# Turned w_out blocks in one PSUM bank with one copy, the first group's logits one piece later, the output's split ahead of the state's sum

## The chip, the cores and the metric

The kernel runs on one core of a Trainium2 chip. The metric is the device time of one execution in microseconds (us). A core has five engines, each with its own in-order queue: PE (TensorE, matrix products; its weight loads are shown as PEld), DVE (VectorE), ACT (ScalarE), POOL (GpSimd) and SP (SyncE, which here only issues DMAs). An engine's next instruction waits behind the one before it. PE writes its results to PSUM, which has eight banks; DVE and ACT read them there, POOL can't.

## What is computed

Three layers, one after the other, on 3072 tokens of width 384.

```
# 1. a linear-attention recurrence over 768 steps (4 batches, 8 heads of 48)
cur   = (u * k_t) outer v_t
y_t   = r_t @ (state + cur)
state = w * state + k_t outer v_t
# 2. a feed-forward layer
h = x @ w_in          # 384 -> 2048
x = maximum(0.01 * h, h) @ w_out      # 2048 -> 384
# 3. routing to one of 8 experts, for tokens with a positive score
score, logits = x @ w_skip, x @ w_gate
e = argmax(logits);  gate = softmax(logits)[e]
out = x + gate * (relu(x @ w1[e]) @ w2[e])     # where score > 0, else out = x
```

## The kernel before, in words

**Number format.** Every product runs in f16 with two parts: a value is split into a high part and a rest, and three products (high by high, rest by high, high by rest) are added in PSUM. "The split" is such a pair: ACT rounds to f16, DVE (or POOL) subtracts.

**Tiling.** The attention runs in 24 steps i of 128 tokens, each in two chunks c of 64. Three steps make a group g of 384 tokens, eight groups in all. One step consists of these functions: `att_S` (PE, line 334, the products of k and r), `take_S` (DVE, L343, the masked copy into `dg`), `att_V` (PE, L358, a chunk's contribution to the state), `next_T` (DVE, L374 adds it to the decayed state `Tw`, L376 decays the sum again), `att_Y` (PE, L391), `att_R` (PE, L406, the state's share of the output) and `take_y` (for each chunk ACT L424 and DVE L425: the output's split into `xt`). From step 8 on, S uses banks 0 and 1, and V, Y and R of both chunks use banks 2 and 3: Y and R the columns below 256, V those above. The listings call banks 0 to 7 bank_85 to bank_92. Some waits between engines are kept by bank, not by column: in the listing of the kernel before, the second L424 waits for the state's sum, which reads other columns of the same bank.

**The feed-forward layer.** `mm1` (L477 to L479) makes 9 products of 384 columns per block f of 16, `mm2` (L505 to L507) 12 per piece q of four f. `mm1` ends in ACT L482 and DVE L483, then ACT L492 and L493 on DVE or POOL. The end of mm2 is ACT L529 and L530 and DVE L533.

**The opening (0 to about 148 us).** Its order is written out by hand: a string `SEQ` of letters, one for each small function, which all engines follow. While attention runs for the first steps, the weights come in as 64-bit words and are converted: 16 chunks of w_in, then 16 of w_out, each by four DVE operations or three and POOL (letters B, C, X, l or h: L202, L205, L210, then L216 on DVE, or L218 on ACT and L219 on POOL) and ACT L211. Letter x is `turn_w_out`: it transposes block c of w_out, three 128x128 tiles of the high part and three of the rest, by PE (L752) into the two banks of `idle_pair()` (the pair that attention isn't using: bank_87 and bank_88, later bank_85 and bank_86), and ACT copies each bank to `slotE` (L753). Letter f is `fuse_logits`: four turned blocks times the router's weights (PE L234, L235), so that mm2 can give the router's nine logits as nine more columns of w_out (393 columns in place of 384). Letter 2 is one f of the first group's mm2, for which w_out block f must be there.

**After the opening.** A loop over groups g issues mm1 and mm2. `tick()` counts pieces, and on every fourth `pump()` issues half an attention step: S of step i with R of step i-1 and, for the engines behind them, `take_S`, `next_T`, `take_y` in `att_posts`; four ticks later V and Y. The first group has no logits from mm2, since the fused columns weren't ready: `first_logits()` computes them from `xT0`, the group's rows turned by three DMAs on SP (L914). It is called in group 1, i = 0, after piece q = 2. `routing(g)` then works on the logits in small steps, one per piece. After the groups come the experts.

Of the kernel before, what the change touches and what calls it, by code (L numbers as in the profile page):

```python
# [10 lines left out]
F16 = mybir.dt.float16  # L11
# [7 lines left out]
P = 128  # L19
# [10 lines left out]
NK = DM // P  # L30
# [30 lines left out]
def kernel(ctx: ExitStack, tc: tile.TileContext, rk, nat, wT, uN, w_in, w_out, wsg,  # L61
                         w1, w2, c_diag, c_mask, c_id48, c_f16, c_route, c_tok, out):
    nc = tc.nc
    v, act, g_, pe, sp = nc.vector, nc.scalar, nc.gpsimd, nc.tensor, nc.sync
# [19 lines left out]
    def ring(k):  # L84
        turns[k] = turns.get(k, -1) + 1
        if k == "mm":
            return bank[4 + turns[k] % state["ring"]]
        return bank[turns[k] % 2][:, 256:]
# [157 lines left out]
    def fuse_logits(c):  # L246

        whole()
        pl = idle_pair()[c % 2] if state["seq"] else ring("at")
        for j in range(4):  # L250
            for k in range(NK):
                two_parts(pl, j, slotE[:, 0, 4 * c + j, k, :], slotE[:, 1, 4 * c + j, k, :], wsg_s[:, :, k, :],
                          k == 0, k == NK - 1)
        fl = rt.tile([P, 4, 9], F32, name="fl")
        add_parts(fl, pl, 4)
        split(w_out_s[:, 0, 4 * c:4 * c + 4, DM:NX], w_out_s[:, 1, 4 * c:4 * c + 4, DM:NX], fl, 1.0 / SR)
# [60 lines left out]
    def idle_pair():  # L317

        i = done["s"]
        assert i - done["e"] < 2 and done["t"] >= 2 * i - 2  # L320
        return bank[2 * (i % 2):2 * (i % 2) + 2]
# [120 lines left out]
    def pump():  # L442

        i = done["y"]
        if done["s"] == i and (i < NST or done["r"] < NST):
            if i < NST:
                if done["c"] <= i:
                    sum_c()
                if done["d"] <= i:
                    set_diag(g_)  # L450
                att_S()
                att_posts.append(take_S)
            if done["r"] < i:
                att_R()
                if done["t"] < 2 * i:
                    att_posts.append(next_T)
                att_posts.append(take_y)
        elif i < NST:
            if i + 1 < NST:
                for x, f in (("a", scale_rk), ("u", mul_ruk), ("n", scale_k)):  # L460
                    if done[x] <= i + 1:
                        f(g_)
            if done["v"] == i:
                att_V()
            att_Y()
            if done["t"] == 2 * i:
                att_posts.append(next_T)
# [276 lines left out]
    def turn_w_out():  # L744

        c = turn("x")
        assert ready["w"] > NF + c
        whole()
        for h, b in enumerate(idle_pair()):
            tp = b[:, :NK * P // 2].bitcast(F16)  # L750
            for k in range(NK):
                pe.transpose(tp[:, k * P:(k + 1) * P], w_out_s[:, h, c, k * P:(k + 1) * P], ident16)  # L752
            act.copy(slotE[:, h, c].rearrange("p k n -> p (k n)"), tp)  # L753

    posts = []

# [104 lines left out]
    for g in range(NG):  # L861
# [54 lines left out]
        for i in range(TPG):  # L916
            st = {}
            for q in range(4):
                tick()
                whole()  # L920
                post = mm2(g, gT, i, 4 * q, 4 * q + 4, st, DM if last else NX)
                if g == 1 and i == 0:

                    held, post = post, None
                skew(post)
                flush()
                if last:
                    if i == 0:
                        if q == 0:
                            for f in range(NF - 3, NF):  # L930
                                late_logits(g, gT, f, bank[3])
                            rts = routing(g)
                        for _ in range(2 if q == 1 else 1):
                            next(rts, None)
                        if q == 1:
                            for k in range(NB2):
                                if k != buf_of(E0, 0):
                                    g_.memset(xg_b[k], 0.0)
                    if (i, q) in ((1, 0), (1, 1), (2, 1)):
                        next(cnts)  # L940
                    if i < 2:
                        split_pieces(1)
                elif g == 1:
                    if i == 0:
                        if q == 2:
                            first_logits()
                        if q == 3:
                            rts = routing(0)
                    else:
                        next(rts, None)  # L950
                    if (i, q) == (1, 3):
                        for j in range(TPG):
                            store_x(0, j)
                        held()
                elif q % 2:
                    if early < 16:
                        pieces.append(load_expert(early // 8, early % 8, stg, NST4))
                        early += 1
                    if len(pieces) > 2 or (pieces and early == 16):
                        pieces.pop(0)()  # L960
# [225 lines left out]
```

## Time and profile before

| | |
|---|---|
| median of three runs | 640.87 us (640.70 to 642.69) |
| the profiled execution | 639.15 us, span 637.3 us from first to last instruction |
| busy share of the span | PE 95%, DVE 66%, ACT 40%, POOL 40% |
| mean granted TensorE clock | 0.991 of full speed |

How to read it: busy times are shares of the span of one profiled execution. PE's busy time is a union of overlapping matmuls (a 384-column matmul lasts 0.33 us but the next starts 0.16 us later). An idle time is written in brackets behind the instruction that ended it, with the instruction that released it. Idle time of an engine other than the one that sets the pace costs nothing by itself.

### The profile page before, as it was taken

The numbers are of one execution on the slowest core, as the hardware profiler recorded it, in microseconds if no ns is written. First come the engines' busy times: TensorE is split into PE (matmuls) and PEld (weight loads), VectorE is DVE, ScalarE is ACT, GpSimd is POOL, SyncE is SP. The second block draws the span as 40 slices with busy tenths as digits, with TensorE's granted clock in tenths as the row PEclk, the third lists the DMA queues.
The fourth block names the chain that finished last, engine by engine and source line by source line (L and its number), as shares of the span: only waits on it lengthen the run. The fifth ranks groups of instructions, "written<-read, shape, count | busy, mean of one in ns | idle before, by whom it ended". The sixth has DMA issues, their size and how long they took to land.

```text
span 637.3 us, 17708 instructions
## 1 busy us (share of the span) xinstructions
PE 603.0 (95%) x7116; PEld 393.1 (62%) x7116; DVE 417.6 (66%) x907; ACT 255.4 (40%) x539; POOL 253.5 (40%) x242
## 2 busy tenths in 40 slices
PE   8899988988999999999999999999999999999994
PEld 4456555655656666665666666666566677777772
DVE  7999988863278738956884892583177363473751
ACT  1236656552045225433642541252155242352530
POOL 3958654543542624544262454421013323221310
PEclk9989999999999999999999999999999999999998
DMA  8867354623632652553263243003155755797750
GB/s 266 252 198 224 91 159 141 192 67 76 138 117 77 169 163 100 155 169 111 68 171 118 89 120 101 14 2 90 35 180 176 242 141 156 238 213 213 188 152 12
DMA packets 60350, 89.04 MB, mean 140 GB/s; under 512 B 20706, under 2 KB 44224, under 8 KB 60240
## 3 DMA queue, kind: packets, MB, share of 16 engines
q1 hardware_dynamic: 56784, 81.64, 44.6%
q0 software_dynamic: 2880, 5.49, 2.9%
q8 instruction: 66, 1.08, 0.7%
q10 hardware_dynamic: 576, 0.47, 0.2%
q14 instruction: 44, 0.36, 0.2%
HBM read 68.86 MB, written 17.23 MB: 135 GB/s over the span
## 4 chain that ended last, share of the span: by engine, by line
PE 50%; DMA 15%; DVE 14%; issue 12%; POOL 5%; ACT 2%; POOLq 0%; SPq 0%; DVEq 0%; ACTq 0%
PE bank L505 8%; PE bank L507 8%; PE bank L506 8%; PE bank L477 7%; PE bank L478 7%; PE bank L479 7%; DMA idxl<-tokid,su 6%; DMA out_x<-y,idx 3%; DMA xg<-xbuf,idx 3%; DVE wc L210 2%; PE bank L406 2%; DVE bank L202 2%; DVE bank L205 2%; PE bank L358 1%; PE bank L334 1%
## 5 line engine op out<-in xcount | busy, mean ns | idle before, releaser
L477 PE MATMUL bank<-xt,slotA 128*128 128x384 f16 x384 | 125.4, 326 | 2.4 <-DVE gg L483 2.3
L479 PE MATMUL bank<-xt,slotA 128*128 128x384 f16 x384 | 125.2, 326 | 0.0
L478 PE MATMUL bank<-xt,slotA 128*128 128x384 f16 x384 | 125.2, 326 | 0.0
L505 PE MATMUL bank<-slotB,slotC 128*128 128x393 f16 (+1 forms) x336 | 110.7, 329 | 0.0
L507 PE MATMUL bank<-slotB,slotC 128*128 128x393 f16 (+1 forms) x336 | 110.5, 329 | 0.0
L506 PE MATMUL bank<-slotB,slotC 128*128 128x393 f16 (+1 forms) x336 | 110.5, 329 | 0.0
L483 DVE TENSOR_TENSOR gg<-bank,gg 128x384 f32<-128x384 f32 x128 | 70.2, 551 | 30.6 <-ACT gg L482 30.3
L482 ACT ACTIVATE gg<-bank 128x384 f32<-128x384 f32 x128 | 61.9, 489 | 60.0 <-PE bank L479 42.6
L493 DVE TENSOR_TENSOR slotC<-gg,slotC 128x384 f16<-128x384 f32 x101 | 78.5, 780 | 0.2
L298 POOL TENSOR_TENSOR dg<-cs,diag 128x512 f32<-128x512 f32 x21 | 22.2, 1057 | 130.9 <-DVE cs L291 130.9
L492 ACT CAST slotC<-gg 128x384 f16<-128x384 f32 x112 | 56.8, 508 | 15.5 <-DVE gg L483 14.8
L533 DVE SCALAR_TENSOR_TENSOR x<-bank,x 128x384 f16<-128x384 f32 x24 | 13.2, 557 | 72.4 <-ACT x L530 69.1
L270 POOL TENSOR_TENSOR raw<-raw,consts 112x512 f32<-112x512 f32 x44 | 56.8, 1315 | 0.1
L478 PEld LDWEIGHTS <-slotA 128*128 128x128 f16 x384 | 37.5, 98 | 25.0 <-issue 3.1
L479 PEld LDWEIGHTS <-slotA 128*128 128x128 f16 x384 | 37.5, 98 | 24.9
L477 PEld LDWEIGHTS <-slotA 128*128 128x128 f16 x384 | 37.4, 97 | 23.8
L529 ACT ACTIVATE x<-bank 128x384 f16<-128x384 f32 x24 | 11.8, 492 | 92.4 <-PE bank L507 79.2
L507 PEld LDWEIGHTS <-slotC 128*128 128x128 f16 x336 | 32.9, 98 | 22.7
L505 PEld LDWEIGHTS <-slotC 128*128 128x128 f16 x336 | 32.8, 98 | 21.9
L506 PEld LDWEIGHTS <-slotC 128*128 128x128 f16 x336 | 32.9, 98 | 20.7
L590 POOL DMA_INDIRECT idxl<-tokid,su x24 | 25.7, 1069 | 50.1 <-DVE s L594 39.6
L992 ACT ACTIVATE h<-bank 128x512 f16<-128x512 f32 x28 | 16.7, 596 | 60.4 <-PE bank L986 44.3
(211 smaller groups left out, 1284.4 us busy)
## 6 DMA issues: line engine op xcount, KB each, us to landing
raw<-in_w SPq DMA_DIRECT2D x48, 384.0 KB, 5.7
raw<-in_nat SPq DMA_DIRECT2D x24, 576.0 KB, 5.8
raw<-in_rk SPq DMA_DIRECT2D x24, 448.0 KB, 4.0
xbuf<-x SPq DMA_DIRECT2D x23, 384.5 KB, 5.8
wst<-in_w_in SPq DMA_DIRECT2D x16, 384.0 KB, 6.7
wst<-in_w_out SPq DMA_DIRECT2D x16, 384.0 KB, 3.5
wst<-in_w SPq DMA_DIRECT2D x16, 384.0 KB, 5.6
out_x<-x SPq DMA_DIRECT2D x24, 192.0 KB, 1.9
```

The source lines that it names most:

```text
L270: eng.tensor_mul(r4[:, a], r4[:, a], tab.unsqueeze(2).broadcast_to([112, NPAIR, 2, C]))
L477: pe.matmul(ph[:, :n], wh, xt[:, 0, k, t0:t0 + n], start=k == 0, stop=False)
L478: pe.matmul(ph[:, :n], wh, xt[:, 1, k, t0:t0 + n], start=False, stop=False)
L479: pe.matmul(ph[:, :n], wl, xt[:, 0, k, t0:t0 + n], start=False, stop=k == NK - 1)
L482: act.activation(gg[:, :n], ph[:, :n], AF.Copy, scale=0.01)
L483: v.tensor_max(gg[:, :n], ph[:, :n], gg[:, :n])
L492: act.copy(gT[:, 0, f, t0:t0 + n], gg[:, :n])
L493: eng.tensor_sub(gT[:, 1, f, t0:t0 + n], gg[:, :n], gT[:, 0, f, t0:t0 + n])
L505: pe.matmul(po[:, :c1 - c0], gh, w_out_s[:, 0, f, c0:c1], start=start, stop=False)
L506: pe.matmul(po[:, :c1 - c0], gh, w_out_s[:, 1, f, c0:c1], start=False, stop=False)
L507: pe.matmul(po[:, :c1 - c0], gl, w_out_s[:, 0, f, c0:c1], start=False, stop=stop)
L590: g_.indirect_dma_start(out=idxl[i], out_offset=bass.IndirectOffsetOnAxis(ap=su[:, i:i + 1], axis=0), in_=tokid[:, ti:ti + 1], in_offset=N ...
```

## The change

Three edits. First, `turn_w_out`: where no V of the step ahead has been issued into the idle pair (`done["v"] <= done["s"]`), all six transposes of block c go into one bank, bank c % 2 of the pair, 768 f16 columns wide, and one ACT copy of 2x384 columns takes both parts to `slotE`. 13 of the 16 blocks are turned so; blocks 3, 4 and 5 keep two half banks and two copies. `fuse_logits` writes to the bank of the block turned last. Second, `first_logits()` is called after piece q = 3. Third, in `pump()` the split `take_y` stands ahead of `next_T`, the state's sum.

```
-        pl = idle_pair()[c % 2] if state["seq"] else ring("at")
+        pl = idle_pair()[(done["x"] + 1) % 2] if state["seq"] else ring("at")
...
                 att_R()
+                att_posts.append(take_y)
                 if done["t"] < 2 * i:
                     att_posts.append(next_T)
-                att_posts.append(take_y)
...
-        for h, b in enumerate(idle_pair()):
-            tp = b[:, :NK * P // 2].bitcast(F16)
+        banks = idle_pair()
+        whole_bank = done["v"] <= done["s"]
+        tps = ([banks[c % 2][:, :NK * P].bitcast(F16)] if whole_bank else
+               [b[:, :NK * P // 2].bitcast(F16) for b in banks])
+        for h in range(2):
+            tp = tps[0][:, h * NK * P:] if whole_bank else tps[h]
             for k in range(NK):
                 pe.transpose(tp[:, k * P:(k + 1) * P], w_out_s[:, h, c, k * P:(k + 1) * P], ident16)
-            act.copy(slotE[:, h, c].rearrange("p k n -> p (k n)"), tp)
+            if not whole_bank:
+                act.copy(slotE[:, h, c].rearrange("p k n -> p (k n)"), tp)
+        if whole_bank:
+            act.copy(slotE[:, :, c].rearrange("p h k n -> p h (k n)"), tps[0].rearrange("p (h n) -> p h n", h=2))
...
-                        if q == 2:
+                        if q == 3:
                             first_logits()
-                        if q == 3:
                             rts = routing(0)
```

On ACT, near the end of the opening (blocks 9 to 13; L211 and L218 belong to the conversion of later chunks, wc is their staging tile), before:

```order
L753 COPY slotE_140<-bank0_85 128x384
L753 COPY slotE_140<-bank1_86 128x384
L753 COPY slotE_140<-bank0_85 128x384
L753 COPY slotE_140<-bank1_86 128x384
L211 ACTIVATE slotB_137<-wc_1895 128x384
L753 COPY slotE_140<-bank0_85 128x384
L753 COPY slotE_140<-bank1_86 128x384
L753 COPY slotE_140<-bank0_85 128x384
L753 COPY slotE_140<-bank1_86 128x384
L211 ACTIVATE slotB_137<-wc_1956 128x384
```

And after:

```order
L492 CAST slotD_139<-gg_1501 128x384
L760 COPY slotE_140<-bank1_86 128x2x384
L760 COPY slotE_140<-bank0_85 128x2x384
L211 ACTIVATE slotB_137<-wc_1887 128x384
L760 COPY slotE_140<-bank1_86 128x2x384
L760 COPY slotE_140<-bank0_85 128x2x384
L211 ACTIVATE slotB_137<-wc_1946 128x384
L218 ACTIVATE wc_1946<-wc_1946 128x384
```

Each pair of copies became one, and two blocks in a row no longer share a bank.

On DVE, the end of step 9 in group 2 (dg and S's banks 85, 86; T, Tw the state; xt the output's two parts; gg the mm1 result), before:

```order
L493 TENSOR_TENSOR slotC<-gg,slotC 128x384
L343 COPY_PREDICATED dg<-mask,bank_85 128x256
L343 COPY_PREDICATED dg<-mask,bank_86 128x256
L374 TENSOR_TENSOR T<-Tw,bank_88 112x192
L376 TENSOR_TENSOR Tw<-T,pw 112x192
L425 SCALAR_TENSOR_TENSOR xt<-bank_87,xt 112x4x64
L425 SCALAR_TENSOR_TENSOR xt<-bank_88,xt 112x4x64
L483 TENSOR_TENSOR gg<-bank_90,gg 128x384
```

And after:

```order
L493 TENSOR_TENSOR slotC<-gg,slotC 128x384
L343 COPY_PREDICATED dg<-mask,bank_85 128x256
L343 COPY_PREDICATED dg<-mask,bank_86 128x256
L425 SCALAR_TENSOR_TENSOR xt<-bank_87,xt 112x4x64
L425 SCALAR_TENSOR_TENSOR xt<-bank_88,xt 112x4x64
L374 TENSOR_TENSOR T<-Tw,bank_88 112x192
L376 TENSOR_TENSOR Tw<-T,pw 112x192
L483 TENSOR_TENSOR gg<-bank_90,gg 128x384
```

The two halves of the output's split moved ahead of the sum and its decay; the rows around them stayed. With that, the second L424 on ACT has no wait for the sum any more.

## Rows read from the trace of the kernel before

**Rows 1.** Stretches: length, busy us (count) by engine, PEclk, DMA share, GB/s.

```profile
100.00:120.00 20.00, 17.77 (x243) 11.66 (x243) 17.01 (x40) 11.38 (x30) 9.95 (x10) 1.00 0.52 156
...
200.00:220.00 20.00, 20.00 (x218) 12.45 (x217) 15.80 (x38) 7.99 (x19) 10.95 (x10) 1.00 0.50 128
...
560.00:580.00 20.00, 19.22 (x250) 15.89 (x250) 10.50 (x15) 6.82 (x11) 5.58 (x5) 1.00 1.04 245
```

**Rows 2.** Waits of PE, 90 to 150 us: total, times, longest.

```profile
PE bank L752 <- ACT slotE L753: 4.4, 5, 1.6
PE bank L234 <- ACT slotE L753: 1.0, 2, 0.6
```

**Rows 3.** Waits of PE, 150 to 485 us.

```profile
PE bank L358 <- POOL ru L278: 1.6, 2, 0.8
PE bank L234 <- DMA slotE<-x: 1.2, 1, 1.2
PE bank L358 <- DVE xt L425: 0.8, 1, 0.8
```

**Rows 4.** PE in order of time, turns and fused logits: start, length, idle before.

```profile
101.41 0.71 PE L752 MATMUL bank<-cf,slotB 128*128 128x128 f16 x6 [1.60 <-ACT slotE L753]
...
130.35 0.71 PE L752 MATMUL bank<-cf,slotB 128*128 128x128 f16 x6 [1.43 <-ACT slotE L753]
...
138.76 0.17 PE L234 MATMUL bank<-wsg_s,slotE 128*128 128x18 f16 x1 [0.40 <-ACT slotE L753]
```

**Rows 5.** ACT in order of time.

```profile
106.54 0.49 ACT L482 ACTIVATE gg<-bank 128x384 f32<-128x384 f32 x1 [0.91 <-PE bank L479]
...
138.23 0.86 ACT L753 COPY slotE<-bank 128x384 f16<-128x384 f16 x2 [0.83 <-PE bank L752]
```

**Rows 6.** DVE in order of time.

```profile
104.44 0.56 DVE L483 TENSOR_TENSOR gg<-bank,gg 128x384 f32<-128x384 f32 x1 [0.51 <-ACT gg L482]
...
107.06 0.56 DVE L483 TENSOR_TENSOR gg<-bank,gg 128x384 f32<-128x384 f32 x1 [0.84 <-ACT gg L482]
107.53 0.54 DVE L210 SCALAR_TENSOR_TENSOR wc<-wst,bank 128x384 uint32<-128x384 uint32 x1
...
135.69 0.55 DVE L210 SCALAR_TENSOR_TENSOR wc<-wst,bank 128x384 uint32<-128x384 uint32 x1
```

**Rows 7.** Groups by shape: count, busy us, mean ns, idle before.

```profile
L753 ACT COPY slotE<-bank 128x384 f16<-128x384 f16 x32 | 13.6, 476 | 5.0 <-PE bank L752 4.8
...
L992 ACT ACTIVATE h<-bank 128x512 f16<-128x512 f32 x28 | 16.7, 596 | 60.4 <-PE bank L986 44.3 <-issue 12.6 <-ACT slotE L191 1.4
```

**Rows 8.** PE in order of time, the first group's logits.

```profile
155.22 0.17 PE L235 MATMUL bank<-wsg_s,slotE 128*128 128x9 f16 x1
156.56 0.18 PE L234 MATMUL bank<-wsg_s,slotE 128*128 128x18 f16 x1 [1.18 <-DMA slotE<-x]
```

**Rows 9.** DVE, then ACT, at the end of step 9.

```profile
184.94 0.77 DVE L343 COPY_PREDICATED dg<-mask,bank 128x256 f32<-128x256 uint32 x2
185.60 0.34 DVE L374 TENSOR_TENSOR T<-Tw,bank 112x192 f32<-112x192 f32 x1
185.97 1.19 DVE L376 TENSOR_TENSOR Tw<-T,pw 112x192 f32<-112x192 f32 x1
187.09 0.74 DVE L425 SCALAR_TENSOR_TENSOR xt<-bank,xt 112x256 f16<-112x256 f32 x2
...
185.97 0.38 ACT L424 ACTIVATE xt<-bank 112x256 f16<-112x256 f32 x1 [2.32 <-DVE T L374]
```

**Rows 10.** PE, V of steps 9, 10 and 22, and the matmul ahead of one.

```profile
170.67 0.57 PE L358 MATMUL bank<-raw 64*48 64x48 f32 x32
...
186.44 0.33 PE L479 MATMUL bank<-xt,slotA 128*128 128x384 f16 x1
187.60 0.81 PE L358 MATMUL bank<-raw 64*48 64x48 f32 x29 [0.83 <-POOL ru L278]
...
412.12 0.76 PE L358 MATMUL bank<-raw 64*48 64x48 f32 x29 [0.85 <-DVE xt L425]
```

## The prediction

> **What bounds the kernel now.** I read the table of stretches first, then PE's waits, then the rows around each wait. Inside the groups (200 to 220 us) PE is busy for all 20.00 us, DVE for 15.80, ACT for 7.99 [rows 1]: PE sets the pace, and a change is worth what it takes from PE's waits. In the opening it is two engines at once: from 100 to 120 us PE has 17.77 and DVE 17.01 of 20 us [rows 1], both in order, and each sometimes waits for the other. So the next view is who PE waits for. Between 90 and 150 us it is the copies of the turned blocks: 4.4 us in five waits of the transposes and 1.0 us in two of the fused logits [rows 2]. Between 150 and 485 us there are four waits only: 1.2 us for the turned rows of the first group, and three of 0.8 us in front of V [rows 3]. Two of these three are put down to POOL's `ru`, but V at 187.60 comes 0.1 us after the first L425 ends (187.09 and about 0.4 of the pair's 0.74), and its later part after the second [rows 9, 10]; the third row names L425 itself [rows 3, 10]. I take L425 for all three.
>
> **Edit 3, the split ahead of the sum.** At 184.94 DVE does the two masked copies, then the sum (L374, 0.34), the decay (L376, 1.19 here), and only then the two L425, from 187.09 to 187.83; the second L424 on ACT waits 2.32 us for the sum as well [rows 9]. PE is through with mm1 at 186.77 (186.44 and 0.33) and stands 0.83 us [rows 10]. V then also runs torn: its first 29 matmuls take 0.81 us where all 32 take 0.57 at 170.67 [rows 10]; start of V to the end of its last three is about 0.28 us longer. One place costs 1.1 us, three cost 0.83 + 0.81 + 0.85 + 3 x 0.28 = 3.3 us. After the change L425 starts at about 185.6, when L374 started, and the pair ends at 186.35; L374 follows to 186.6, and the long L376 is behind everything that V needs. V on the first bank is free at 186.0 and on the second, whose state columns the sum must have read, at 186.65, when PE arrives at 186.7. Gain 3.3 us; the most that is left is about 0.1 at each place. Nobody else is late: the sum ends before the L425 did, ACT loses a wait, SP's `xt` DMAs behind L425 go earlier.
>
> **Edit 2, logits one piece later.** PE does two thirds of the logits up to 155.22 and begins the last third at 156.56, when the third turning DMA lands [rows 8]: 1.3 us lost beyond the 0.03 pitch. One piece is 12 matmuls at 0.167 us, 2.0 us. Put ahead, it ends at about 157.0, and the last third comes 0.7 us after the data. Gain 1.3 us, and it needs the DMAs to move with PE, which they do, since the rows they turn come from mm2. What goes later: DVE's first routing steps, by 0.8 us on the old clock; the next use of them on PE is a piece later still. Bounds 0.6 (if the DMA stays where it was in time while PE comes 2.7 us earlier) and 1.3.
>
> **Edit 1, the copies.** Its parts in order.
> - Price of a copy: two copies of 384 columns take 0.86 us as a pair [rows 5]. One of 768 isn't in the trace; from 384 columns at 476 ns [rows 7] and the slope between 476 and 596 ns for 128 more (0.94 ns a column at most), 0.80 to 0.84 us. So ACT gains nothing worth a term; 13 instructions go, 40% busy stays. A copy starts after six transposes and not after three, 0.17 us later, which counts where PE waits for it.
> - Block 2 at 101.41 waited 1.60 us for block 1's copies in the same banks [rows 4]. It now goes to the other bank, and PE is 1.6 us earlier, 2.0 with the torn second half. DVE at that time stands for ACT's L482, which stands for PE (106.54 after 0.91 idle [rows 5]; the three L483 at 104.44 to 107.06 after 0.51, 0.66 and 0.84 [rows 6]). With PE ahead these three run at their own pitch of 0.47: 104.4, 104.85, 105.3, and L210 comes at 105.8 in place of 107.53. **DVE gains 1.7 us**, and from there to the last L210 at 135.69 [rows 6] it has hardly an idle place, so it keeps them.
> - From 107 to 128 us PE follows DVE (the copies stand behind ACT's L211, which waits for L210), 1.7 us earlier.
> - Block 10 at 130.35 waited 1.43 us for block 9's copies [rows 4]: gone, PE is 3.1 us ahead, then 3.5 with block 12's 0.4.
> - Then a new wait takes part back. The third fused logits write into the bank of block 13, turned last, and wait for its whole copy. That stands behind the L211 of the last chunk, whose L210 ends at 136.24 - 1.7 = 134.5: L211, then the copy from 135.05 to 135.9. Before, they began at 138.76 [rows 4]: 2.8 us gained, with PE idle for about 2 us ahead of it.
> - Block 15's copy begins after six transposes: 0.1 us lost on the way to `dg` and step 8's end.
>
> Sum of edit 1: **2.7 us**. Lower bound: if DVE doesn't keep the 1.7 us, the third logits come at 137.65 and 1.0 us is left; if alternating gave nothing at all, the full copy (138.23 + 0.84, where the first half was enough) and block 15 would cost 0.4. Upper bound 3.5, without the new wait. I take 2.7: each row on the way names the engine ahead of it.
>
> The page "Perfetto Trace Analysis" of the Trainium skill (section "Optimizing Scalar/DVE Operations") says that grouping operations pays where the engine is saturated, and gives about 51 ns of ScalarE overhead on PSUM. By that, 13 copies less give an estimated 0.7 us on an engine that isn't saturated, and nothing of the time; the rows agree that ACT isn't what is short.
>
> **The sum.** 3.3 + 1.3 + 2.7 = 7.3 us. Against the profiled execution: 639.15 - 7.3 = 631.85 us (span 630.0). The other three runs lie 1.5 to 3.5 us above the profiled one, with the median 640.87, so the forecast for the median is 640.87 - 7.3 = 633.6 us. Bounds of the parts: 3.0 to 3.5, 0.6 to 1.3, -0.4 to 3.5.
>
> **Rivals.**
> - *DVE doesn't keep its lead* (it is at 17 of 20 us, and its operations grow where POOL works beside them): edit 1 gives 1.0, total 5.6, 635.3 us. For it: the length of L376, 1.19 here [rows 9]. Against: DVE's idle places in 104 to 107 us are plainly waits for PE. Chance 0.15.
> - *The wait changes sides.* L424 and the sum read the same bank and can't overlap; now the sum waits for L424 and L425, and V waits for the sum. If the sum (or the decay with it) came as late as the L425 did, the three places would stay: 4.0 us gained, 636.9 us. Against: the 1.19 us decay is behind the sum. Chance 0.08. The page "PSUM — Partial Sum Buffer" of the Trainium skill (section "PSUM bank collisions raise a hardware error") says that two engines must be kept apart on one bank and quadrant, reads against reads included; that is the wait of 2.32 us [rows 9], and by that rule the order is turned and the exclusion stays.
> - *The wins are taken back later.* Between 560 and 580 us the DMA queues show a share of 1.04 [rows 1]. If the experts' weights set the end, an earlier PE waits there, and the time is 640.9 us. Against: PE is busy 19.22 us in that stretch, and the weight loads are issued when buffers are read, so they move with PE. Both this and the first two in part: about 638.5. Chance 0.10 for all of it.
> - *Slower: DVE waits at the head of its queue.* In 13 steps DVE now reaches L425 first, which needs R and ACT, where it used to do sum and decay (0.34 + about 0.36 at least) in that time. If DVE stands 0.7 us in each with the L483 of mm1 behind it, and PE then lacks a free bank, that is 13 x 0.7 = 9.1 us, and V's waits stay: 640.87 - 4.0 + 9.1 = 646.0 us. It decides once L483 is as late as PE's need of the bank; between 150 and 485 us PE waits for no L483 [rows 3], and DVE has some 4 us in 20 to spare [rows 1]. Chance 0.05.
> - *The edits do nothing:* the order of instructions shows each where it is meant to be, so this is only the third rival.
>
> **How the numbers follow.** The forecast, all three parts, has 0.62. The range reaches from 631.0 (all upper bounds, 8.3 us, off the profiled execution) over the first two rivals to 637.5 and leaves out the 0.10 of the third and 0.05 of the slower one. Two versions are told apart from about 0.3%, 1.9 us, so faster means below 638.95: 0.62 + 0.15 + 0.08 and 0.03 of the third rival's partial case, 0.88. Same 0.07, slower 0.05.
>
> **What would show it.** Edit 3: V of steps 10, 16 and 22 at about 182.8, 293.9 and 405.1 us (187.60 less 4.0 and 0.83, then 1.1 more each time) without an idle time, and L425 ahead of L374. Edit 2: no wait for `slotE<-x`. Edit 1: no wait of blocks 2 and 10, the last L210 near 134.0, the third fused logits near 136.0 behind a wait of about 2 us. Wrong would be a last L210 that stays near 135.7 (first rival), V waiting for T (second), new waits of PE in mm1 for L483 (the slower one), or a gain by 450 us that is gone at the end (third).

## The result and the profile after

The changed kernel takes 635.99 us (median of four runs, 634.5 to 637.52) where the kernel before took 641.78 in the same comparison: ratio 0.9895, 95% interval 0.9859 to 0.9932. Two later batches gave 0.9913 (0.9883 to 0.9944) and 0.9878 (0.9846 to 0.9909). So it is about 1% faster, 5.8 us. The forecast was 633.6 us, with a range of 631.0 to 637.5: the direction is right, the time is in the range, and the gain is 1.5 us short of the 7.3 us forecast.

The profiled execution of after took 636.7 us, with a span of 634.8. Its opening ran 2.74 us late before any of the three edits acts: the first block of `w_out` is turned at 94.76 us, against 92.02 before. In fourteen profiles of this study that point lies between 92.0 and 95.1 us. From there up to the third fused logits two profiles of one kernel agree to some hundredths of a microsecond, so below I count from block 0's first transpose. In the changed kernel L756 are the transposes, L758 the half copies, L760 the joined copy, and L477 to L507 the mm1 and mm2 matmuls as before.

The table of stretches of after (length, busy us and count of PE, PEld, DVE, ACT and POOL, then PEclk, DMA share, GB/s):

```profile
100.00:120.00 20.00, 18.96 (x255) 12.45 (x253) 18.66 (x43) 12.66 (x31) 11.56 (x12) 1.00 0.57 177
139.00:142.00 3.00, 3.00 (x23) 1.79 (x20) 1.32 (x5) 0.24 (x1) 0.00 (x0) 0.59 0.20 80
142.00:145.00 3.00, 3.00 (x23) 1.90 (x22) 0.00 (x0) 1.28 (x2) 0.00 (x0) 0.84 0.00 0
200.00:220.00 20.00, 20.00 (x218) 12.41 (x217) 15.75 (x37) 7.92 (x17) 11.93 (x11) 1.00 0.46 115
```

Against [rows 1], PE and DVE both work more of the stretch from 100 to 120 us, and the groups are as they were. New at this place is PEclk, the granted share of TensorE's full clock: 0.59 and 0.84 between 139 and 145 us. PE counts as busy there for every microsecond, and yet it is slow. PE's waits of after between 90 and 150 us (total, times, longest):

```profile
PE bank L234 <- ACT slotE L760: 3.0, 2, 1.8
PE bank L756 <- ACT slotE L758: 0.9, 1, 0.9
PE bank L477 <- DVE gg L483: 0.7, 1, 0.7
PE bank L234 <- DVE dg L343: 0.6, 1, 0.6
```

Of the 4.4 us of the transposes in [rows 2], 0.9 is left, ahead of a block that kept its half banks; the fused logits (L234) went from 1.0 to 3.0 us. From 150 to 485 us the same view of after is empty: all four waits of [rows 3] are gone. PE of after in order of time, at the places of [rows 4], [rows 8] and [rows 10]:

```profile
102.39 0.50 PE L756 MATMUL bank<-cf,slotB 128*128 128x128 f16 x6
...
126.57 0.17 PE L234 MATMUL bank<-wsg_s,slotE 128*128 128x18 f16 x1 [1.21 <-ACT slotE L760]
...
129.34 0.83 PE L756 MATMUL bank<-cf,slotB 128*128 128x128 f16 x12
...
138.46 0.17 PE L234 MATMUL bank<-wsg_s,slotE 128*128 128x18 f16 x1 [1.75 <-ACT slotE L760]
...
139.22 0.32 PE L506 MATMUL bank<-slotB,slotC 128*128 128x384 f16 x1
139.38 0.37 PE L507 MATMUL bank<-slotB,slotC 128*128 128x384 f16 x1
139.55 0.53 PE L505 MATMUL bank<-slotB,slotC 128*128 128x384 f16 x1
139.87 0.53 PE L506 MATMUL bank<-slotB,slotC 128*128 128x384 f16 x1
...
158.41 0.17 PE L234 MATMUL bank<-wsg_s,slotE 128*128 128x18 f16 x1
...
186.84 0.57 PE L358 MATMUL bank<-raw 64*48 64x48 f32 x32
```

Block 2 (102.39) has no wait, blocks 9 and 10 run in one piece of twelve transposes (129.34), the first group's logits (158.41) and V of step 10 (186.84) start without a wait, and V is whole, 32 matmuls in 0.57 us. The third fused logits stand 1.75 us for the copy of the block turned last. Half a microsecond after them the starts of the mm2 matmuls go from 0.16 us apart (139.22, 139.38) to 0.32 (139.55, 139.87), half of the rate, until 142.75. I call this the slow stretch. DVE of after in order of time, the last L210 and the split:

```profile
136.61 0.55 DVE L210 SCALAR_TENSOR_TENSOR wc<-wst,bank 128x384 uint32<-128x384 uint32 x1
...
185.71 0.74 DVE L425 SCALAR_TENSOR_TENSOR xt<-bank,xt 112x256 f16<-112x256 f32 x2
186.37 0.34 DVE L374 TENSOR_TENSOR T<-Tw,bank 112x192 f32<-112x192 f32 x1
186.75 0.53 DVE L376 TENSOR_TENSOR Tw<-T,pw 112x192 f32<-112x192 f32 x1
```

The joined copy's group by shape on ACT (count, busy us, mean ns, idle before):

```profile
L760 ACT COPY slotE<-bank 128x768 f16<-128x768 f16 x13 | 10.0, 793 | 4.3 <-PE bank L756 4.3
```

The last L210 is 1.8 us earlier, counted from block 0 (43.67 to 41.85). The split starts right behind the masked copies, in the place that the sum had before [rows 9], and the sum and the decay follow behind it. A whole copy takes 793 ns, where a pair of halves took 0.86 us [rows 5].

### The profile page after: what moved, and what is told of

It is laid out like the page before. It is cut to its first block, busy times and chain, and to the rows that moved or that the text cites. A ratio compares the mean times of both kernels' runs of the same rounds, so it can differ in the third digit from the quotient of the medians.

```text
span 634.8 us, 17710 instructions
## 1 busy us (share of the span) xinstructions
PE 603.1 (95%) x7116; PEld 392.4 (62%) x7116; DVE 417.3 (66%) x907; ACT 255.4 (40%) x526; POOL 253.9 (40%) x242
## 5 line engine op out<-in xcount | busy, mean ns | idle before, releaser
L477 PE MATMUL bank<-xt,slotA 128*128 128x384 f16 x384 | 125.3, 326 | 3.0 <-DVE gg L483 2.9
L507 PE MATMUL bank<-slotB,slotC 128*128 128x393 f16 (+1 forms) x336 | 111.0, 330 | 0.0
L483 DVE TENSOR_TENSOR gg<-bank,gg 128x384 f32<-128x384 f32 x128 | 70.0, 551 | 27.2 <-ACT gg L482 26.8
L477 PEld LDWEIGHTS <-slotA 128*128 128x128 f16 x384 | 37.5, 98 | 23.8
L529 ACT ACTIVATE x<-bank 128x384 f16<-128x384 f32 x24 | 11.8, 492 | 95.1 <-PE bank L507 75.8
L507 PEld LDWEIGHTS <-slotC 128*128 128x128 f16 x336 | 33.0, 98 | 23.0 <-issue 0.5
```

What stands on the lines that cost most here:

```text
L477: pe.matmul(ph[:, :n], wh, xt[:, 0, k, t0:t0 + n], start=k == 0, stop=False)
L483: v.tensor_max(gg[:, :n], ph[:, :n], gg[:, :n])
L507: pe.matmul(po[:, :c1 - c0], gl, w_out_s[:, 0, f, c0:c1], start=False, stop=stop)
```

## The experiments

Three batches of kernels, the runs of one batch on one chip, and a last run by itself. Times are medians, with the ratio to the kernel before in the same batch:

| kernel | us | before | ratio (95%) |
|---|---|---|---|
| e1, edit 1 alone | 640.95 | 643.44 | 0.9967 (0.9945 to 0.9990) |
| e2, edits 2 and 3 | 639.17 | 643.44 | 0.9928 (0.9901 to 0.9954) |
| e3, logits in the other bank | 632.27 | 643.44 | 0.9829 (0.9800 to 0.9858) |
| e4, wait filled | 635.17 | 643.44 | 0.9866 (0.9839 to 0.9894) |
| e5, changed kernel | 634.27 | 639.53 | 0.9913 (0.9883 to 0.9944) |
| e6, two copies | 633.69 | 639.53 | 0.9905 (0.9879 to 0.9931) |
| e7, one bank | 635.06 | 639.53 | 0.9931 (0.9904 to 0.9957) |
| e8, sum first | 632.62 | 639.53 | 0.9890 (0.9862 to 0.9918) |
| e10, logits in the other bank | 629.16 | 639.95 | 0.9820 (0.9792 to 0.9847) |
| e11, changed kernel | 632.18 | 639.95 | 0.9878 (0.9846 to 0.9909) |
| e12, wait filled | 633.36 | 640.39 | 0.9878 (0.9836 to 0.9920) |

e9, the kernel before, was executed once, for its profile (639.15 us).

The intervals are 3 to 5 us wide, wider than most of the steps in question. The traces are sharper. Each has the same marks, here in us from block 0's first transpose to the start of the mark (of V, to the end of the last one), and in the last column from there to the end of the span:

| profile | block 2 | last L210 | third logits | block 15 | last V | rest |
|---|---|---|---|---|---|---|
| before | 9.39 | 43.67 | 46.74 | 50.60 | 341.92 | 203.4 |
| e9, before | 9.39 | 43.68 | 46.75 | 50.61 | 341.25 | 203.3 |
| e2, edits 2 and 3 | 9.39 | 43.69 | 46.76 | 50.62 | 337.36 | 208.1 |
| e7, one bank | 9.71 | 43.39 | 46.27 | 50.14 | 337.19 | 202.4 |
| after | 7.63 | 41.85 | 43.70 | 49.23 | 335.96 | 204.1 |
| e5, changed kernel | 7.63 | 41.83 | 43.68 | 49.10 | 335.82 | 202.7 |
| e11, changed kernel | 7.63 | 41.82 | 43.67 | 47.53 | 334.43 | 202.7 |
| e1, edit 1 alone | 7.63 | 41.83 | 43.67 | 49.21 | 340.81 | 206.8 |
| e8, sum first | 7.64 | 41.83 | 43.68 | 49.21 | 337.69 | 205.3 |
| e6, two copies | 7.63 | 42.01 | 43.92 | 49.45 | 336.36 | 203.5 |
| e4, wait filled | 7.64 | 41.85 | 43.70 | 47.56 | 334.38 | 206.2 |
| e12, wait filled | 7.63 | 41.83 | 43.68 | 47.54 | 334.64 | 202.4 |
| e3, other bank | 7.63 | 41.49 | 40.42 | 44.28 | 331.35 | 207.1 |
| e10, other bank | 7.63 | 41.48 | 40.42 | 44.28 | 331.38 | 202.3 |

**e1, edit 1 alone.** Edits 2 and 3 undone in the changed kernel.

```
-                att_posts.append(take_y)
                 if done["t"] < 2 * i:
                     att_posts.append(next_T)
+                att_posts.append(take_y)
...
-                        if q == 3:
+                        if q == 2:
                             first_logits()
+                        if q == 3:
```

> Edit 1 alone (edits 2 and 3 undone). Theory (a new wait and then half the clock): the third fused logits stand about 1.7 us for the copy of the block turned last, and about 1 us later the second third of the following mm2 matmuls comes at 0.32 us in place of 0.16 us each, with a granted clock under 0.7 in that 3-us stretch; edit 1 is then worth 1.3 us: time before less 1.0 to 1.6 us, and V of steps 10, 16 and 22 waits 0.8 us each as before. Rival A (the forecast's step, the wait alone and the slow stretch of the after run an accident of that one run): the wait is there, the clock is 1.00 behind it, and 2.7 us or more are gained. Rival B (edit 1 does nothing that lasts): 0 +- 0.4.

Block 15 came 1.39 us earlier than before, the last V 1.11 us. The time's interval (0.6 to 3.5 us gained) holds both theories. The trace doesn't: the wait of 1.76 us is there, and so is the slow clock. The stretch behind the logits in e1:

```profile
138.40:141.40 3.00, 3.00 (x15) 1.82 (x14) 0.86 (x3) 0.80 (x1) 0.00 (x0) 0.50 0.05 18
```

PEclk is 0.50, the lower of the two levels (1.2 of 2.4 GHz). PE's waits from 150 to 485 us are those of [rows 3] again, 1.7 and 0.9 us in front of V and 1.3 us for the turned rows. So the slow stretch of after wasn't an accident of one execution, and edit 1 alone is enough for it to come.

**e2, edits 2 and 3.** The kernel before, with `first_logits()` one piece later and `take_y` ahead of `next_T`; `turn_w_out` and `fuse_logits` as before.

> Edits 2 and 3 on the kernel before (edit 1 undone). Theory: the three V waits gone (3.4 us) and the wait for the first group's turned rows gone (1.2 to 1.3 us): 4.6 to 4.7 us less than before; the clock between the third fused logits and block 15 stays 1.00. If edit 2's DMA stays where it was in time, 4.0 to 4.2. Rival (edit 1 carried part of edit 3's or edit 2's gain, since PE comes earlier there): the difference to before is under 3.5 us.

The last V ends 4.56 us earlier than before (341.92 to 337.36), and the time agrees (ratio 0.9928, 4.6 us). The opening stays as it was to 0.02 us, block 15 at 50.62, PEclk 1.00. V of step 9 starts at 77.36 from block 0 and at 78.65 before, which is edit 2's 1.29 us; the other 3.27 us are edit 3's. The view of PE's waits from 150 to 485 us is empty. The two edits don't lean on edit 1. POOL and PE of e2 at step 10:

```profile
185.74 0.99 POOL L278 TENSOR_TENSOR ru<-ru,consts 128x384 f32<-128x384 f32 x1
```

```profile
186.43 0.59 PE L358 MATMUL bank<-raw 64*48 64x48 f32 x32
```

V starts 0.3 us before POOL's `ru` is finished (186.73), so V doesn't wait for it, although [rows 3] puts two of the three stalls down to it.

**e3, the logits in the other bank.** The changed kernel, with the fused logits not in the bank of the block turned last but in that of the block turned second last.

```
-        pl = idle_pair()[(done["x"] + 1) % 2] if state["seq"] else ring("at")
+        pl = idle_pair()[done["x"] % 2] if state["seq"] else ring("at")
```

> The changed kernel with the fused logits in the other bank of the pair, that of the block turned second last, whose copy is done at about 135.0 us of the changed kernel's profile while PE arrives at 136.7. Theory (the wait costs 1.7 us and the half clock behind it another 1.7 us): third fused logits at about 136.9 in place of 138.46, no wait of over 0.3 us ahead of them, mm2 behind them at 0.16 us, block 15 about 3.3 us earlier than 143.99; 3.0 to 3.4 us less than the changed kernel, so 8.5 to 9.3 us less than before. The second fused logits lose their wait of 1.21 us too, but PE follows DVE there: 0. Rival A (the slow mm2 belong to that stretch itself, whatever stands ahead): 1.6 us less than the changed kernel, clock again under 0.7. Rival B (the time goes into the next wait, for POOL's dg ahead of the fourth logits): the wait of 0.58 us there grows to 2 us or more and under 1 us is gained.

PE of e3, block 13 and the third fused logits:

```profile
132.36 0.50 PE L756 MATMUL bank<-cf,slotB 128*128 128x128 f16 x6
132.69 0.17 PE L234 MATMUL bank<-wsg_s,slotE 128*128 128x18 f16 x1
```

The logits follow the transposes at the transposes' own pace, without a wait, and the clock stays at 1.00. Block 15 comes 4.95 us earlier than in after (49.23 to 44.28), more than the 3.3 us expected: 1.67 to 1.70 us is the half clock (below), and the third logits themselves come 3.28 us earlier, not 1.6. The rest stems from the second fused logits. They lost their wait of 1.21 us too, and blocks 9 and 10 then start at 33.22 instead of 34.58. My expectation put nothing down for that, because I had PE following DVE there. The wait for `dg` ahead of the fourth logits is 0.58 us as in after, so rival B falls.

**e4 and e12, the wait filled.** Seven matmuls that nobody reads, 512 columns each, ahead of the third fused logits; the wait for the copy stays.

```
         assert done["x"] >= 4 * c + 4
+        if c == 2:
+            warm(7, done["x"] % 2, 4 * P)
         fuse_logits(c)
```

> The changed kernel with seven matmuls of 512 columns that nobody reads, into the bank that is free, right ahead of the third fused logits: PE works in its wait of 1.75 us, and the wait for the copy stays where it was. Theory (PE's idle time of 1.75 us is what lowers the clock): the logits start at 138.4 to 138.6 us as before this edit, the mm2 behind them come at 0.16 us, clock 1.00, block 15 at about 142.3 in place of 143.99: 1.4 to 1.8 us less than the changed kernel, 7.2 to 7.6 less than before. Rival (the slow mm2 have another cause): 0 +- 0.3 against the changed kernel, clock again under 0.7.

> The changed kernel with seven unread matmuls in the wait ahead of the third fused logits, a second time, since in one of the three profiles of the changed kernel the half clock did not come although the wait of 1.75 us was there. Over all kernels with that wait empty it came in five of six profiles. Theory (PE's idle time brings it on): none here either, block 15 at 47.5 to 47.6 us from block 0, last V's end at 334.4; by chance alone two filled profiles without it would be 1 in 36. Rival (it comes and goes with that stretch, whatever PE does in the wait): half clock again, block 15 at 49.1 to 49.3. Time: 6.5 to 7.7 us less than before.

PE of e12, then its stretches behind the logits:

```profile
135.60 0.50 PE L756 MATMUL bank<-cf,slotB 128*128 128x128 f16 x6
135.93 1.67 PE L107 MATMUL bank<-wu 128*128 128x512 f16 x7
137.85 0.17 PE L234 MATMUL bank<-wsg_s,slotE 128*128 128x18 f16 x1 [0.24 <-ACT slotE L760]
```

```profile
139.00:142.00 3.00, 3.00 (x28) 2.03 (x27) 1.05 (x4) 1.04 (x2) 0.00 (x0) 1.00 0.13 50
142.00:145.00 3.00, 3.00 (x50) 1.89 (x48) 0.00 (x0) 1.85 (x5) 1.47 (x3) 1.00 0.00 0
```

The logits start at 43.68 from block 0, exactly as in the changed kernel: the copy sets them, whatever PE does. But the clock stays at 1.00, and block 15 is at 47.54 and 47.56 instead of 49.10 to 49.23. PE did useless work, and by block 15 the kernel was 1.6 us ahead of the executions with the slow stretch. The whole times don't show this gain: e12's ratio to before is that of e11, the changed kernel (0.9878 both). The medians are 8.3 us (e4) and 7.0 us (e12) below before, where I had said 7.2 to 7.6 and 6.5 to 7.7.

**e5 and e11, the changed kernel again.**

> The changed kernel once more, with a profile of its own. Counted from block 0 of the turned blocks, which took the opening's variation out of the five profiles seen so far to within 0.03 us: block 2 at 7.63, last L210 at 41.85, third fused logits at 43.70 behind a wait of 1.75, then a stretch of half clock, block 15 at 49.2, last V at 335.4. If the half clock belongs to the wait it comes again; if it was an accident of one run, block 15 is at 47.6. The time from the last V to the end, 203.9 to 208.7 us in the profiles so far, can't be told beforehand; if the changed kernel gave back its gain there, it would be longer than the 203.9 of the kernel before by the 6 us gained, if not, anywhere among these. Time: 5.5 to 7.0 us less than before.

> The changed kernel, for the comparison side by side: from block 0, third fused logits at 43.7 behind a wait of 1.75 us, half clock behind it, block 15 at 49.1 to 49.3, last V's end at 335.8 to 336.0; 5.5 to 6.5 us less than before.

The third fused logits of e11, then one stretch behind the logits from each, e5 first and then e11:

```profile
136.33 0.17 PE L234 MATMUL bank<-wsg_s,slotE 128*128 128x18 f16 x1 [1.75 <-ACT slotE L760]
```

```profile
138.00:141.00 3.00, 3.00 (x14) 1.64 (x13) 1.30 (x5) 0.24 (x1) 0.00 (x0) 0.52 0.10 38
```

```profile
137.00:140.00 3.00, 3.00 (x27) 1.93 (x24) 1.32 (x5) 1.04 (x2) 0.00 (x0) 1.00 0.28 112
```

e5 repeats after. e11 doesn't, and my expectation missed: it has the same wait of 1.75 us and the full clock behind it, block 15 at 47.53, and its median is 7.8 us below before where I had said 5.5 to 6.5. So the same kernel has the slow stretch in some executions and not in others, and 49.10 to 49.23 against 47.53 is what it costs: 1.6 to 1.7 us. Over all kernels that wait there with PE empty (after, e1, e5, e6, e8, e11) it came in five profiles of six, and in none of the eight others. Five in six is a count of profiles and no rate: the mean granted clock of a run, which takes in every low stretch of it, is 0.987 to 0.991 in five of e5's six runs (633.75 to 635.93 us; the sixth has 0.993 and 631.41), and 0.992 or 0.993 in five of e11's six (631.44 to 632.27 us; the sixth has 0.988 and 635.41). With e3 and e10, where the wait is gone, and e4 and e12, where it is filled, I take PE's idle time as what brings it on. For the filling this is argued more than shown: by the counts alone, none of two against five of six comes about by chance once in nine. And the idle time isn't enough for it: e7 has a wait of 1.97 us ahead of other work (below), before has 1.60 and 1.43 [rows 4], all with PEclk at 1.00 behind them. What else decides stays open. The Trainium skill, page "TensorE: Matmul & The Clock Gate" (section "Part 1: The HAM clock gate (the "warmup" mystery)"), says that the clock has only these two levels; the 0.50 of e1 agrees with that. It also says that the number of matmuls that a kernel starts with at the lower one differs from run to run; e5 and e11 differ in a like way, but in the middle of the kernel.

**e6, two copies.** The changed kernel, with its packed and alternating banks, but two copies of 384 columns from each whole bank.

```
-            act.copy(slotE[:, :, c].rearrange("p h k n -> p h (k n)"), tps[0].rearrange("p (h n) -> p h n", h=2))
+            for h in range(2):
+                act.copy(slotE[:, h, c].rearrange("p k n -> p (k n)"), tps[0][:, h * NK * P:(h + 1) * NK * P])
```

> The changed kernel with its packed, alternating banks, but two copies of 384 columns for each whole block in place of one of 768. Theory (alternating the banks is edit 1's gain, joining the copies is worth next to nothing, since ACT is busy for half of the time): block 2 at 7.6 us from block 0, block 15 at 49.2 to 49.5, the wait ahead of the third fused logits 1.7 to 1.9 and the half clock behind it as in the changed kernel; time within 0.5 us of it, 5.3 to 6.8 us less than before. Rival (fewer instructions on ACT pay: 13 x (0.86 - 0.80) = 0.8 us, and 13 semaphores): block 15 at 50.0 or later.

Block 15 is at 49.45, 0.2 to 0.35 us later than in the changed kernel's executions with the slow stretch, with the third logits 0.2 us later and the same slow stretch. The time can't be told from that of e5 (633.69 and 634.27). Joining the copies is worth a quarter of a microsecond on the path; the rest of edit 1 is the choice of banks.

**e7, one bank.** The changed kernel with whole blocks always in the first bank of the pair, and the fused logits always in the second.

```
-        tps = ([banks[c % 2][:, :NK * P].bitcast(F16)] if whole_bank else
+        tps = ([banks[0][:, :NK * P].bitcast(F16)] if whole_bank else
...
-        pl = idle_pair()[(done["x"] + 1) % 2] if state["seq"] else ring("at")
+        pl = idle_pair()[1] if state["seq"] else ring("at")
```

> The changed kernel with one joined copy for each whole block, but always in the first bank of the pair, and the fused logits in the second, where no block's copy stands in their way. Theory (alternating is what pays): block 2 waits for block 1's whole copy and comes at 9.3 to 9.7 us from block 0 (7.63 with alternating banks, 9.39 before), block 10 at 38.2 to 38.8 (34.58, 38.33), third fused logits right behind block 13 at 46.2 to 46.8, no half clock, block 15 at 50.2 to 50.9; what is left are edits 2 and 3: 4.0 to 4.9 us less than before. Rival (packing or joining carries part of the gain): block 15 at 49.6 or earlier.

PE of e7 at block 10, and its waits from 90 to 150 us:

```profile
132.20 0.49 PE L756 MATMUL bank<-cf,slotB 128*128 128x128 f16 x6 [1.97 <-ACT slotE L760]
```

```profile
PE bank L756 <- ACT slotE L760: 5.4, 4, 2.0
PE bank L756 <- ACT slotE L758: 0.7, 1, 0.7
```

Nearly all is back where it was before, and a little longer for each block, since the copy starts after six transposes. Block 15 at 50.14 is 0.46 us better than before, the last V 0.17 better than e2's. Alternating is what pays.

**e8, the sum first.** The changed kernel with sum, split, decay in place of split, sum, decay (the decay of `next_T` is kept back and issued behind `take_y`).

```
-                att_posts.append(take_y)
+                late = []
                 if done["t"] < 2 * i:
-                    att_posts.append(next_T)
+                    att_posts.append(lambda: next_T(v, late))
+                att_posts.append(take_y)
+                att_posts.append(lambda: late and late.pop()())
```

> The changed kernel with the state's sum ahead of the output's split again, and only the decay behind it. Theory (the decay of 0.53 to 1.19 us was what held the split up, the sum of 0.34 us fits in ahead of PE's arrival): L425's pair ends 0.36 us later than in the changed kernel, at about 186.7 us of the old clock where PE arrives at 186.77; V of steps 10, 16 and 22 without a wait or with one of up to 0.1 us, last V within 0.3 us of 335.4 from block 0. Rival A (each operation ahead of the split costs its length): waits of 0.3 us, and a torn V, 0.3 to 0.6 us each: last V 0.9 to 1.8 us later. Rival B (the three stalls came from POOL's ru, as two of the rows name it): no difference between this order and either of the others could be explained; V waits as in the kernel before, 3.3 us later.

DVE of e8 at step 15 (L429 is the split there), then V of step 16 on PE:

```profile
298.66 0.34 DVE L374 TENSOR_TENSOR T<-Tw,bank 112x192 f32<-112x192 f32 x1
298.93 0.95 DVE L429 SCALAR_TENSOR_TENSOR xt<-bank,xt 112x256 f16<-112x256 f32 x2
299.79 0.44 DVE L376 TENSOR_TENSOR Tw<-T,pw 112x192 f32<-112x192 f32 x1
```

```profile
299.78 0.67 PE L358 MATMUL bank<-raw 64*48 64x48 f32 x29
300.26 0.23 PE L395 MATMUL bank<-dg,raw 64*64 64x64 f32 x1
300.28 0.22 PE L358 MATMUL bank<-raw 64*48 64x48 f32 x3
```

V starts without a wait, so POOL's `ru` isn't what held it (rival B), and the decay was what pushed the split too late. But V is torn in 29 and 3, as the second half of the split isn't through: 0.72 us from start to end instead of 0.57, which is 0.10 to 0.15 us at each of three places. That is less than rival A's 0.3 to 0.6. The last V is 1.8 us later than in the changed kernel, where I had allowed 0.3; 1.3 of that is one wait of mm1 for the routing's `lg` at 179.56 us. Whether this order caused it is open: e8's profiled execution took 639.79 us while the other six runs took 631.37 to 634.45, at a mean clock of 0.990 to 0.994 where the profiled one had 0.984, and the median is no longer than the changed kernel's.

**e9 and e10, side by side with e11.** The kernel before, and e3's kernel, again.

> The kernel before once more, for a second profile of its own. From block 0 of the turned blocks: block 2 at 9.39, third fused logits at 46.74, block 15 at 50.6, the three stalls of V 0.8 to 0.9 us each, last V's end at 341.9, each within 0.1 us. The stretch from the last V's end to the end of the span was 203.4 us in the first profile and 202.4 to 208.1 in the nine profiles of the other kernels, 206.2 to 208.1 in the four of one batch and 202.4 to 205.3 in the four of the other. If it goes by the chip or the moment, this run and the two beside it agree within about 2.5 us whatever kernel they run; if the changed kernels gave their gain back there, theirs are 5 us or more longer than this one.

> The changed kernel with the fused logits in the bank of the block turned second last, again, side by side with the changed kernel itself: block 15 at 44.3 us from block 0, last V's end at 331.3, no half clock; 4.4 to 4.6 us less than the changed kernel and 10 to 11 less than before. If the first run's advantage was the batch's, under 2 us less than the changed kernel.

From the last V to the end e9 has 203.3, e10 202.3 and e11 202.7 us: the same, though the last V of e10 comes 9.9 us earlier (counted from block 0) than that of e9. In the first batch that stretch was 206.2 to 208.1 us in all four kernels. It goes by the batch and the execution, not by the edits. e10 repeats e3's marks to 0.03 us and is 3.0 us below the changed kernel (629.16 and 632.18). I had expected 4.4 to 4.6, which holds against an execution with the slow stretch (335.82 less 331.38); e11 had none, and against it the traces say 3.05. PE's waits of e9 from 150 to 485 us:

```profile
PE bank L234 <- DMA slotE<-x: 1.3, 1, 1.3
PE bank L358 <- DVE xt L425: 0.8, 1, 0.8
PE bank L358 <- POOL ru L278: 0.8, 1, 0.8
```

Here the kernel before had two stalls of V and not three: at step 10 the decay took 0.39 us where it took 1.19 in [rows 9], and the split was through in time. (The last V is only 0.67 us earlier for it, not 1.1, since PE came to step 10 about 0.4 us late in e9.) So edit 3 is worth two stalls or three, 2.2 or 3.3 us, by the execution. POOL's rows show what made the decay long. First POOL of before, beside the decay at 185.97 in [rows 9], then POOL and DVE of e9:

```profile
185.95 1.00 POOL L278 TENSOR_TENSOR ru<-ru,consts 128x384 f32<-128x384 f32 x1
```

```profile
183.83 2.82 POOL L270 TENSOR_TENSOR raw<-raw,consts 112x512 f32<-112x512 f32 x2
```

```profile
186.48 0.39 DVE L376 TENSOR_TENSOR Tw<-T,pw 112x192 f32<-112x192 f32 x1
```

The decay ends about 0.2 us after the POOL operation that was running when it started: in before POOL ends at 186.95 and the decay at 187.16, in e9 at 186.65 and 186.87. It is so at all 98 places behind 150 us, seven in each of the fourteen profiles, where POOL works beside the decay; at the 304 others the decay takes 0.35 to 0.36 us. In before the decay starts 0.02 us behind the start of `ru` at steps 10, 16 and 22, and these are the three stalls.

## Why the prediction was right, and where it was off

- **What bounds the kernel.** Right. The waits of [rows 2] and [rows 3] that were taken away were on the path, and what stands behind them moved.
- **Edit 3**, forecast 3.3 us, of three stalls. Measured 3.27 (e2 against before); in after the gain steps up by 1.14, 1.11 and 1.11 us at the three places. L425 and not POOL was the releaser, as taken (e2, e8), but POOL's `ru` is what held L425 up, through the long decay, as the first rival's remark on DVE beside POOL had it. V of step 10 starts without a wait, and no new wait of PE appears between 150 and 485 us. That there were three stalls to take away and not two belongs to the profiled execution (e9), and there was luck in it.
- **Edit 2**, forecast 1.3 us, measured 1.29 (e2). The logits of after show no wait at 158.41.
- **Edit 1**, forecast 2.7 us. Step by step: block 2 and block 10 without a wait, as said; DVE keeps 1.8 us (1.7 said); third logits 3.04 us earlier (2.8 said) behind a wait of 1.75 us (2 said). The mechanism was right up to there. **The step that failed is the last term, "then a new wait takes part back".** It was sized as the idle time alone. In five of six profiles with this wait PE's clock then fell to its lower level, which cost another 1.6 to 1.7 us by block 15. With it edit 1 is worth 1.4 to 1.5 us there (50.60 to 49.10 or 49.23), without it 3.07 (e11). In [rows 1] PEclk was 1.00 in each stretch, and I asked nowhere what a longer wait would do to it. The trace of before had an answer in its opening, in a stretch that isn't in [rows 1]:

```profile
31.26 1.30 PE L334 MATMUL bank<-raw 48*64 48x64 f32 x29 [1.95 <-POOL ru L278]
```

```profile
31.00:38.00 7.00, 6.74 (x103) 4.41 (x104) 6.57 (x15) 2.83 (x7) 4.54 (x6) 0.53 0.75 198
```

Behind a wait of 1.95 us PE worked at about half of the clock for nearly 7 us. A wait of 2 us, as forecast, had that price beside it. (It isn't always paid there either: e6 has such waits of 1.95 and 1.92 us in its opening, with the clock at 1.00 up to 137 us.)

- **"From 107 to 128 us PE follows DVE"** was wrong too, with less effect on the sum. The second fused logits' wait grew from 0.59 to 1.21 us, and it lay on the path: e3 without it has blocks 9 and 10 1.36 us earlier, with DVE's last L210 only 0.36 us earlier. PE was held by ACT's copies there, not by DVE's pace. For the same reason the upper bound of 3.5 us "without the new wait" was too low: e3 gains 6.32 us by block 15.
- **The joined copy** was forecast as no term on ACT, and it is one of 0.2 to 0.35 us by block 15 (e6, one profile). The Trainium skill, page "Perfetto Trace Analysis" (section "Optimizing Scalar/DVE Operations"), has grouping pay where the engine is saturated; ACT isn't, and this small gain comes through PE's waits for single copies, 0.86 to 0.79 us each.
- **The sum.** 3.3 + 1.3 + 1.4 = 6.0 us, and the last V of after ends 5.96 us earlier. The median of 635.99 lies 2.4 us above 633.6: 1.3 us of it is what edit 1 fell short in the trace (1.4 in place of 2.7), and 0.9 that the runs of before had a median of 641.78 in this comparison and not 640.87. The lower end of the range, 631.0, is a little off its own sum: 639.15 less 8.3 is 630.85.
- **The rivals.** DVE kept its lead; V doesn't wait for the sum; PE waits for no L483 between 150 and 485 us in after, so the slower case is out. "Taken back later" is out by e9 to e11: the stretch behind the last V shows no relation to the gain.

## What to carry to other kernels

Where three users share two PSUM banks, give the third the bank whose copy is already done, not the one filled last: this one subscript is worth 3.0 us beside the changed kernel in the same batch, and makes a version faster than both (ratio to before 0.9820 and 0.9829). When a change moves several short waits of PE into one longer one, price that wait with the clock behind it, and if it can't be removed, unread matmuls in it can be cheaper than nothing (by the traces of e4 and e12; two profiles). When an operation takes three times its usual time in one place, look at what the other engines run beside it: the decay's 1.19 us ended with POOL's operation, and moving the split ahead of the decay cured the stall without touching POOL. And where steps of 1 or 2 us are in question, count from a mark just ahead of the edits: from there these traces agree to a few hundredths of a microsecond over the next 45 us and to 0.7 us at the last V where the clock is the same, while the whole times of one kernel scatter over 3 us and more.

## What the hardware showed that I had not expected

- After PE had stood 1.75 to 1.81 us and begun 24 narrow matmuls that take 0.6 us, the granted clock went to 0.50 for about 3 us, with PE busy all that time, in five profiles of six. It fell 0.4 us (e5) to 1.5 us (e1, e8) after the first of them. The mm2 starts were 0.32 us apart instead of 0.16. Seven matmuls of 512 columns in the wait kept the clock at 1.00 both times.
- The wait alone doesn't decide it: one of the six kept its clock (e11), and so did PE behind a wait of 1.97 us in e7.
- The same decay on DVE (L376, 112x192) at the same place of the kernel before took 1.19 us in one execution and 0.39 in another. With the long one V of step 10 stalled, with the short one it didn't. It ended 0.2 us after the POOL operation that was running when it started, at all 98 places where there was one.
